# Reordering the opening of a fused retention and GELU kernel, and starting one attention stage a unit of the first layer later

## The chip, the cores and the metric

One core of one Trainium2 chip. The metric is the time of one execution in microseconds (us) on the device. A trace gives the span from the first to the last instruction; it is 1.6 to 1.9 us shorter than the time of the same execution.

## The reference, cut to what matters

```python
# attention: q, k, v of shape (4, 8, 768, 64), a decayed running state for each head
for t in range(S):
    state = gamma * state + einsum('bhd,bhe->bhde', k[:, :, t], v[:, :, t])
    y[:, :, t] = scale * einsum('bhd,bhde->bhe', q[:, :, t], state)
x = y.transpose(0, 2, 1, 3).reshape(3072, 512)
# then a two-layer network with w_in (512 x 2048) and w_out (2048 x 512)
h = x @ w_in
out = gelu_tanh(h) @ w_out
```

The kernel cuts the sequence into six chunks of 128 steps. In each chunk there are four tiles, one for each of the four batches. For a tile it computes: transposes of q and k (T), the masked products of k and q (A), the chunk's output y from A and v plus the old state times q, and the new state s. The four tiles of a chunk then go through the first layer (M1, into banks called h), GELU on ScalarE, and the second layer (M2, into banks called o). While a chunk is in M1 and M2, the attention of the next chunk is woven in between.

## The kernel before

The parts that the argument needs, with cuts marked:

```python
    def prep1(eng, nm, c, b):          # decay factors times q or k, or a plain cast of v, to fp16
        ...
    BANKS = {"h": 2, "o": 2, "att": 4} # PSUM banks of each kind
    ...
    def spin(n, tag="h"):              # products of zeros, to keep TensorE busy
        ps = bank(tag, shape=(128, 512), name="spin_ps")
        for _ in range(n):
            nc.tensor.matmul(out=ps, lhsT=zero[:, 0:128], rhs=zero, start=True, stop=True)
    ...
    # loads of chunk 0: q, k, v of four tiles from the queues of SyncE and ScalarE; then, in program order:
    spin(14)
    prep1(VE, "q", 0, 0)
    prep1(PO, "k", 0, 0)               # GpSimd
    mm_T(0, 0)
    ev_T(0, 0, AC)                     # eviction on ScalarE
    load1(AC, "v", 0, 2)
    prep1(VE, "q", 0, 1)
    prep1(PO, "k", 0, 1)
    prep1(PO, "k", 0, 2)

    load_w_in(0)                       # first w_in block, half of the contraction each,
    load_w_in(1)                       # both issued by GpSimd, behind its k of tile 2
    prep1(PO, "k", 0, 3)
    ... # further w_in, w_out; then A, y, T, A ... of tiles 0 to 3 with spins between
    t01, t23 = (0, half), (half, 2 * half)
    m1a = [moe1_parts(0, fp, *t01) for fp in range(2)]
    m1a[0](range(2))                   # M1 of tiles 0 and 1, first half of the contraction: load_w_in(0)
    ...
    m1a[0](range(2, 4))                # second half: needs load_w_in(1)
    m1a[1](range(2, 4))
    for b in range(2):
        ev_S(0, b)
        moe1_two(0, b, *t23)           # M1 of tiles 2 and 3, in an h bank
        mm_s(0, 2 + b)
    ...
    # SyncE's loads of chunk 1 begin when w_out part 2 has landed (hold), all in one queue:
    hold("q", 1, 1, w_out_sb[2][0:1, 0, 0:1])
    ...
    for b in range(B):
        load1(SY, "k", 2, b)
    load_blk("q", 2)                   # sixteen transfers: q of chunk 2, all tiles
    ...
    for nm in "kqv":                   # GpSimd: k of chunk 2, then q, then v
        for b in range(B):
            prep_blk("q", 2, b) if nm == "q" else prep1(PO, nm, 2, b)
    # M1 of chunk 1, sixteen units; after unit n comes the attention of chunk 2:
            8: [(att_T, 2, 0), (load, 3)],
            10: [(att_T, 2, 1)],
            13: [(att_AY, 2, (), "att", 2, (0, 1), None)],   # A of tiles 0 and 1
```

Of the kernel before, what the change touches and what calls it, by code (L numbers as in the profile page):

```python
# [16 lines left out]
def kernel(  # L17
# [40 lines left out]
    att = ctx.enter_context(tc.tile_pool(name="att", bufs=4))  # L58
# [30 lines left out]
    def ld_tile(nm, c, b):  # L89
        if nm == "q":  # L90
            t = ld_all(("q32", c)).rearrange("p (b hp) a d -> p b (hp a d)", b=B)
            return t[:, b].rearrange("p (h d) -> p h d", h=H)
        if (nm, c, b) not in raw:
            raw[nm, c, b] = ld.tile([128, H, Dh], F32, tag=f"{nm}32", bufs=6, name=f"{nm}32")
        return raw[nm, c, b]
# [72 lines left out]
    def spin(n, tag="h"):  # L168
        ps = bank(tag, shape=(128, 512), name="spin_ps")
        for _ in range(n):  # L170
            nc.tensor.matmul(  # L171
                out=ps, lhsT=zero[:, 0:128], rhs=zero, start=True, stop=True
            )
# [9 lines left out]
    def prep1(eng, nm, c, b):  # L183
        t = pre.tile(
            [128, H, Dh], F16, tag=f"{nm}16", bufs=6 if nm == "q" else 2 * B, name=f"{nm}16"
        )
        src = ld_tile(nm, c, b)
        if nm == "v":
            if eng is nc.scalar:
                eng.copy(out=t, in_=src)  # L190
            else:
                eng.tensor_copy(out=t, in_=src)
        else:
            col = OQ if nm == "q" else OK
            eng.tensor_tensor(  # L195
                out=t,
                in0=src,
                in1=cst[:, col:col + H].unsqueeze(2).broadcast_to([128, H, Dh]),
                op=ALU.mult,
            )  # L200
        h16[nm, c, b] = t
# [12 lines left out]
    def pair(t, hp):  # L214
        return t[:, 2 * hp:2 * hp + 2]
# [6 lines left out]
    def copy_on(eng, out, in_):  # L222
        if eng is nc.scalar:
            eng.copy(out=out, in_=in_)  # L224
        else:
            eng.tensor_copy(out=out, in_=in_)  # L226
# [5 lines left out]
    def bank(tag, dt=F32, shape=(128, NHP, 128), name="ps"):  # L232
        return psum.tile(list(shape), dt, tag=tag, bufs=BANKS[tag], name=name)

    def mm_T(c, b):
        parts = [(i, nm) for i, nm in enumerate("qk") if c not in BLK[nm]]
        if not parts:
            return
        ps = bank("att", F16, (128, 2, NHP, 128), "qkT_ps")
        for i, nm in parts:  # L240
            for hp in range(NHP):
                nc.tensor.transpose(  # L242
                    out=ps[:, i, hp], in_=pair(h16[nm, c, b], hp), identity=iden
                )
        pss["T", c, b] = ps

    def ev_T(c, b, eng=nc.vector):
        t = att.tile([128, 2, NHP, 128], F16, tag="qkT", name="qkT")
        for i, nm in enumerate("qk"):
            if c in BLK[nm]:  # L250
                nc.vector.transpose(  # L251
                    out=t[:, i].rearrange("p hp t -> p (hp t)"),
                    in_=blk16.pop((nm, c, b)).rearrange("p ha d -> p (ha d)"),
                )
        if ("T", c, b) in pss:
            i0 = sum(c in BLK[nm] for nm in "qk")
            copy_on(eng, t[:, i0:], pss.pop(("T", c, b))[:, i0:])
        qkT[c, b] = t

    def mm_A(c, b):  # L260
        t = qkT[c, b]
        ps = [bank("att", name=f"a_ps{j}") for j in range(2)]
        for hp in range(NHP):
            for j in range(2):
                nc.tensor.matmul(  # L265
                    out=ps[j][:, hp],
                    lhsT=t[j * 64:(j + 1) * 64, 1, hp],
                    rhs=t[j * 64:(j + 1) * 64, 0, hp],
                    start=True,
                    stop=True,  # L270
                )
        pss["A", c, b] = ps

    def ev_A(c, b):
        ps = pss.pop(("A", c, b))
        for j in range(2):
            s = att.tile([128, NHP, 128], F16, tag=f"a{j}", name=f"a_sb{j}")
            nc.vector.tensor_tensor(out=s, in0=ps[j], in1=mask[:, j], op=ALU.mult)  # L278
            a_sb[c, b, j] = s

    def mm_yc(c, b, tag):
        y_ps = pss["Y", c, b] = bank(tag, name="y_ps")
        if c == 0:
            return

        for hp in range(NHP):
            nc.tensor.matmul(  # L287
                out=y_ps[:, hp],
                lhsT=st[:, hp, b],
                rhs=qkT[c, b][:, 0, hp],  # L290
                start=(hp == 0),
                stop=False,
                skip_group_check=True,
            )

    def mm_yi(c, b):
        y_ps = pss["Y", c, b]
        for hp in range(NHP):
            for j in range(2):
                nc.tensor.matmul(  # L300
                    out=y_ps[j * 64:(j + 1) * 64, hp],
                    lhsT=h16["v", c, b][:, 2 * hp + j],
                    rhs=a_sb[c, b, j][:, hp],
                    start=(c == 0),
                    stop=True,
                    skip_group_check=True,
                )

    def ev_Y(c, b, eng=nc.vector):
        if c not in xT:  # L310
            xT[c] = xp.tile([128, NHP, B * C], F16, tag="x", name="xT")
        copy_on(eng, xT[c][:, :, b * C:(b + 1) * C], pss.pop(("Y", c, b)))

    def mm_s(c, b, tag="att"):
        if c + 1 >= NCk:
            return
        s_ps = pss["S", c, b] = bank(tag, name="s_ps")
        for hp in range(NHP):
            nc.tensor.matmul(  # L319
                out=s_ps[:, hp],  # L320
                lhsT=pair(h16["k", c, b], hp),
                rhs=pair(h16["v", c, b], hp),
                start=True,
                stop=True,
            )
# [97 lines left out]
    def moe1_mm(c, fc, out, t0, t1, kcs=range(NHP), first=True):  # L423
        for kc in kcs:
            nc.tensor.matmul(  # L425
                out=out,
                lhsT=w_in_of(fc, kc),
                rhs=xT[c][:, kc, t0:t1],
                start=(kc == 0 and first),
                stop=(kc == NHP - 1),  # L430
                skip_group_check=True,
            )

    def g_tile(c, fc):
        if (c, fc // 2) not in g_sb:
            g_sb[c, fc // 2] = gp.tile([128, 2, B * C], F16, tag=f"g{fc // 2}", name="g")
        return g_sb[c, fc // 2]

    def gelu(out, in_):
        nc.scalar.activation(out=out, in_=in_, func=AF.Gelu_apprx_tanh, scale=1.0)  # L440
# [6 lines left out]
    def moe1_two(c, fp, t0, t1, tag="h"):  # L447

        h_ps = bank(tag, shape=(128, 2, B * C // 2), name="h_ps")
        for r in range(2):  # L450
            moe1_mm(c, 2 * fp + r, h_ps[:, r, 0:t1 - t0], t0, t1)
        gelu(g_tile(c, 2 * fp)[:, :, t0:t1], h_ps[:, :, 0:t1 - t0])
# [64 lines left out]
    VE, AC, PO, SY = nc.vector, nc.scalar, nc.gpsimd, nc.sync  # L517
# [4 lines left out]
    load1(AC, "k", 0, 3)  # L522
    spin(14)
    prep1(VE, "q", 0, 0)
    prep1(PO, "k", 0, 0)
    mm_T(0, 0)
    ev_T(0, 0, AC)
    load1(AC, "v", 0, 2)
# [18 lines left out]
    spin(3)  # L547
    mm_A(0, 1)
    ev_A(0, 1)
    prep1(AC, "v", 0, 1)  # L550
    prep1(VE, "q", 0, 3)
    mm_yc(0, 0, "o")
    mm_yi(0, 0)
    ev_Y(0, 0, AC)
    spin(4)
    mm_yc(0, 1, "o")
    mm_yi(0, 1)
    ev_Y(0, 1, AC)
    mm_T(0, 2)
    ev_T(0, 2)  # L560
    mm_T(0, 3)
    ev_T(0, 3, AC)
    mm_A(0, 2)
    ev_A(0, 2)
    prep1(AC, "v", 0, 2)
    prep1(AC, "v", 0, 3)
    spin(3)
    mm_A(0, 3)
    ev_A(0, 3)


    t01, t23 = (0, half), (half, 2 * half)
    m1a = [moe1_parts(0, fp, *t01) for fp in range(2)]
    m1a[0](range(2))
    mm_yc(0, 2, "o")
    mm_yi(0, 2)
    ev_Y(0, 2, AC)
    m1a[1](range(2))
    mm_s(0, 0)
    mm_s(0, 1)  # L580
    mm_yc(0, 3, "o")
    mm_yi(0, 3)
    ev_Y(0, 3)
    m1a[0](range(2, 4))
    m1a[1](range(2, 4))
    for b in range(2):
        ev_S(0, b)
        moe1_two(0, b, *t23)
        mm_s(0, 2 + b)
    ev_S(0, 2)  # L590
    ev_S(0, 3)
# [52 lines left out]
    for nm in "kqv":  # L644
        for b in range(B):
# [11 lines left out]
            6: [(att_S, 1, 3)],  # L657
            8: [(att_T, 2, 0), (load, 3)],
            10: [(att_T, 2, 1)],
            13: [(att_AY, 2, (), "att", 2, (0, 1), None)],  # L660
            14: [(att_T, 2, 2)],
            15: [(att_T, 2, 3)],
        },
    )
    run(
        [x for b in range(B) for x in units2(1, b)],
        {
            1: [(att_AY, 2, (), "att", 2, (2, 3), None)],
            4: [(att_Y, 2)],
            6: [(att_S, 2, 0)],  # L670
            7: [(att_S, 2, 1)],
            8: [(att_S, 2, 2)],
            9: [(att_S, 2, 3)],
        },
    )

# [60 lines left out]
```

## Time and profile before

| | before |
|---|---|
| time, median of 3 | 213.74 us (213.71 to 213.85) |
| span of the traced execution (its time 214.22 us) | 212.4 us |
| TensorE busy | 205.6 us, 97% |
| spins | 28 matmuls of 128x512 zeros |
| first 128x512 row of M1 / first matmul of M2 | 21.50 / 31.86 us |
| last matmul ends | 208.58 us |

How to read it: TensorE is the bound, and its matmuls stand in program order, so time can only be won where TensorE waits or spins. The view of waits lists the waits by what ended them; the timeline shows when each group of matmuls started. The page and the lines that matter are shown in the prediction below. The **chain that ended last** follows, from the last instruction backwards, what released each step; where it leaves TensorE, something else sets the pace. And a **landing** is the moment when the last of a transfer's sixteen parts has signalled (the records hold sixteen signals for a transfer). The **relay** is the opening's chain of handoffs: TensorE's products, their eviction by ScalarE or VectorE, and the next products that need them.

### The profile page before, as it was taken

To read this page: it belongs to the slowest core of one execution; us is meant where nothing else is said; L and a number is where in the kernel's file an instruction comes from. 1 tells how busy PE (TensorE), PEld (TensorE's weight loads), DVE (VectorE), ACT (ScalarE), POOL (GpSimd) and SP (SyncE) were. 2 spreads that over 40 slices of the span, in tenths; PEclk is the share of its full clock that TensorE was granted. 3 is DMA by queue.
4 is the path that set the end of the run, shared out by engine and by line. 5 is a ranking of instruction groups with operands and counts; after the bars stand their busy time and mean duration, and the time that the engine had idled before them with its cause. 6 is when DMAs were issued, how large, how long until landed. Compare 5 with 4: busy or idle time off the path is not lost.

```text
span 212.4 us, 3868 instructions
## 1 busy us (share of the span) xinstructions
PE 205.6 (97%) x1516; PEld 111.3 (52%) x1516; DVE 89.2 (42%) x161; ACT 84.2 (40%) x141; POOL 95.8 (45%) x117
## 2 busy tenths in 40 slices
PE   7989999999999999999999999999999999999992
PEld 2457444457897564444464444464444464444461
DVE  5478201198619753365544365544355520100001
ACT  2374661255455131465131465131465131565110
POOL 2796400513819418599309599301599301100000
PEclk9999999999999999999999999999999999999999
DMA  6999999999789788979789996879910012100121
GB/s 157 288 250 207 206 203 233 241 241 231 127 222 224 112 161 159 252 177 175 120 162 190 303 192 103 124 153 241 281 34 3 0 49 102 49 0 0 49 92 59
DMA packets 124289, 32.78 MB, mean 154 GB/s; under 512 B 118064, under 2 KB 122416, under 8 KB 124272
## 3 DMA queue, kind: packets, MB, share of 16 engines
q1 hardware_dynamic: 108880, 20.75, 49.4%
q0 software_dynamic: 5600, 8.65, 17.2%
q10 hardware_dynamic: 9792, 3.15, 6.1%
q8 instruction: 12, 0.20, 0.4%
q14 instruction: 5, 0.04, 0.1%
HBM read 30.44 MB, written 6.29 MB: 173 GB/s over the span
## 4 chain that ended last, share of the span: by engine, by line
PE 87%; SPq 4%; DVE 2%; DMA 2%; ACT 1%; issue 1%; POOL 0%; POOLq 0%
PE o_ps L470 39%; PE h_ps L425 34%; SPq L110 4%; PE spin_ps L171 4%; PE a_ps L265 3%; PE y_ps L300 3%; PE y_ps L287 2%; DMA q<-in_q_dram 2%; PE s_ps L319 2%; PE qkT_ps L242 2%; ACT qkT L224 1%; DVE qkT L226 1%; DVE qkT L251 1%; POOL q L206 0%; DVE q L195 0%
## 5 line engine op out<-in xcount | busy, mean ns | idle before, releaser
L470 PE MATMUL o_ps<-w_out,g 128*128 128x512 f16 (+1 forms) x400 | 88.1, 371 | 0.0
L425 PE MATMUL h_ps<-xT,w_in 128*128 128x512 f16 (+1 forms) x464 | 86.8, 342 | 0.3 <-ACT g L440 0.2
L440 ACT ACTIVATE g<-h_ps 128x512 f16<-128x512 f32 x96 | 57.2, 597 | 47.8 <-PE h_ps L425 47.8
L425 PEld LDWEIGHTS <-w_in 128*128 128x128 f16 x464 | 44.4, 98 | 37.9 <-issue 0.3
L470 PEld LDWEIGHTS <-g 128*128 128x128 f16 x400 | 37.7, 98 | 38.8
L278 DVE TENSOR_TENSOR a_sb<-a_ps,mask 128x512 f16<-128x512 f32 x48 | 30.0, 682 | 15.9 <-PE a_ps L265 15.8
L492 ACT COPY o_sb<-o_ps 128x512 f32<-128x512 f32 x19 | 11.1, 586 | 54.3 <-PE o_ps L470 49.9
L497 POOL DMA_DIRECT2D out_dram<-o_sb x17 | 9.6, 564 | 46.9 <-ACT o_sb L492 35.0
L195 POOL TENSOR_TENSOR k<-k,cst 128x512 f16<-128x512 f32 x24 | 24.7, 1036 | 11.9 <-DMA k<-in_k_dram 11.8
L345 POOL TENSOR_TENSOR stg<-st,cst 128x512 f32<-128x512 f16 x16 | 16.3, 1041 | 11.5 <-DVE st L336 9.5
L206 POOL TENSOR_TENSOR q<-q,cst 128x512 f16<-128x512 f32 x16 | 16.6, 1048 | 5.2 <-DMA q<-in_q_dram 5.1
L336 DVE TENSOR_TENSOR st<-s_ps,stg 64x256 f16<-64x256 f32 x32 | 13.5, 422 | 7.8 <-PE s_ps L319 7.3
L251 DVE STREAM_TRANSPOSE qkT<-q 128x512 f16<-128x512 f16 x16 | 11.3, 706 | 11.7 <-POOL q L206 11.7
L195 DVE TENSOR_TENSOR q<-q,cst 128x512 f16<-128x512 f32 x8 | 6.3, 781 | 17.2 <-DMA q<-in_q_dram 17.2
L206 POOL TENSOR_TENSOR kT<-kT,cst 128x512 f16<-128x512 f32 x12 | 12.5, 1044 | 0.0
L226 DVE CAST xT<-y_ps 128x512 f16<-128x512 f32 x11 | 7.2, 686 | 11.9 <-PE y_ps L300 11.9
L508 DVE COPY o_sb<-o_ps 128x256 f32<-128x256 f32 x2 | 0.8, 424 | 26.6 <-PE o_ps L470 26.6
L224 ACT CAST xT<-y_ps 128x512 f16<-128x512 f32 x13 | 7.2, 588 | 9.9 <-PE y_ps L300 9.9
L171 PE MATMUL spin_ps<-zero 128*128 128x512 f16 x28 | 9.6, 499 | 1.3 <-DVE zero L139 1.3
L490 DVE COPY o_sb<-o_ps 128x512 f32<-128x512 f32 x4 | 2.8, 691 | 19.0 <-PE o_ps L470 14.7
L265 PE MATMUL a_ps<-qkT 64*128 64x128 f16 x192 | 8.3, 218 | 1.3 <-ACT qkT L224 0.7
L251 DVE STREAM_TRANSPOSE qkT<-kT 128x512 f16<-128x512 f16 x12 | 8.4, 700 | 2.6 <-POOL kT L206 2.6
(32 smaller groups left out, 98.2 us busy)
## 6 DMA issues: line engine op xcount, KB each, us to landing
v<-in_v_dram SPq DMA_DIRECT2D x22, 256.0 KB, 4.4
k<-in_k_dram SPq DMA_DIRECT2D x20, 256.0 KB, 4.9
out_dram<-o_sb POOLq DMA_DIRECT2D x17, 256.0 KB, 3.2
q<-in_q_dram SPq DMA_DIRECT2D x64, 64.0 KB, 2.7
kT<-in_k_dram SPq DMA_DIRECT2D x48, 64.0 KB, 2.7
w_out<-in_moe_w_out_dram POOLq DMA_DIRECT2D x4, 512.0 KB, 15.5
w_in<-in_moe_w_in_dram POOLq DMA_DIRECT2D x3, 512.0 KB, 8.9
q<-in_q_dram SPq DMA_DIRECT2D x5, 256.0 KB, 6.1
```

The costliest lines, as they stand in the source:

```text
L171: nc.tensor.matmul(out=ps, lhsT=zero[:, 0:128], rhs=zero, start=True, stop=True)
L195: eng.tensor_tensor(out=t, in0=src, in1=cst[:, col:col + H].unsqueeze(2).broadcast_to([128, H, Dh]), op=ALU.mult,)
L206: nc.gpsimd.tensor_tensor(out=t, in0=ld_all((key, c))[:, b * NHP:(b + 1) * NHP].rearrange("p hp a d -> p (hp a) d"), in1=cst[:, col:col + ...
L251: nc.vector.transpose(out=t[:, i].rearrange("p hp t -> p (hp t)"), in_=blk16.pop((nm, c, b)).rearrange("p ha d -> p (ha d)"),)
L265: nc.tensor.matmul(out=ps[j][:, hp], lhsT=t[j * 64:(j + 1) * 64, 1, hp], rhs=t[j * 64:(j + 1) * 64, 0, hp], start=True, stop=True,)
L278: nc.vector.tensor_tensor(out=s, in0=ps[j], in1=mask[:, j], op=ALU.mult)
L336: eng.tensor_tensor(out=st[sl, :, b, sl], in0=s_ps[sl, :, sl], in1=stg[sl, :, b, sl], op=ALU.add,)
L345: nc.gpsimd.tensor_tensor(out=stg[:, :, b], in0=st[:, :, b], in1=cst[:, OG:OG + NHP].unsqueeze(2).broadcast_to([128, NHP, 128]), op=ALU.mult,)
L425: nc.tensor.matmul(out=out, lhsT=w_in_of(fc, kc), rhs=xT[c][:, kc, t0:t1], start=(kc == 0 and first), stop=(kc == NHP - 1), skip_group_che ...
L440: nc.scalar.activation(out=out, in_=in_, func=AF.Gelu_apprx_tanh, scale=1.0)
L470: nc.tensor.matmul(out=ps[:, n0:n1], lhsT=g_sb[c, fc // 2][:, fc % 2, b * C:(b + 1) * C], rhs=w_out_sb[fc // (NF // NO)][:, fc % (NF // NO ...
L492: nc.scalar.copy(out=o_sb, in_=ps)
```

## The change

Three parts: (1) k of tile 0 is prepared on VectorE instead of GpSimd; (2) the opening is reordered: T of tile 2 goes ahead of y of tile 1, A of tile 2 ahead of T of tile 3, the s tiles are spread out, the spins are dealt anew (30 instead of 28), and M1 of tiles 2 and 3 takes one o bank so that it needn't wait for a GELU; (3) A of chunk 2, tiles 0 and 1, goes behind unit 14 of M1 instead of unit 13, and all that follows in chunk 2 moves along.

```diff
@@ -522,7 +522,7 @@
     load1(AC, "k", 0, 3)
     spin(14)
     prep1(VE, "q", 0, 0)
-    prep1(PO, "k", 0, 0)
+    prep1(VE, "k", 0, 0)
     mm_T(0, 0)
     ev_T(0, 0, AC)
     load1(AC, "v", 0, 2)
@@ -547,45 +547,46 @@
     spin(3)
     mm_A(0, 1)
     ev_A(0, 1)
-    prep1(AC, "v", 0, 1)
-    prep1(VE, "q", 0, 3)
     mm_yc(0, 0, "o")
     mm_yi(0, 0)
     ev_Y(0, 0, AC)
-    spin(4)
+    prep1(AC, "v", 0, 1)
+    mm_T(0, 2)
+    ev_T(0, 2)
+    spin(3)
     mm_yc(0, 1, "o")
     mm_yi(0, 1)
     ev_Y(0, 1, AC)
-    mm_T(0, 2)
-    ev_T(0, 2)
+    mm_A(0, 2)
+    prep1(VE, "q", 0, 3)
+    ev_A(0, 2)
+    spin(2)
     mm_T(0, 3)
     ev_T(0, 3, AC)
-    mm_A(0, 2)
-    ev_A(0, 2)
+    spin(4)
+    mm_A(0, 3)
+    ev_A(0, 3)
     prep1(AC, "v", 0, 2)
     prep1(AC, "v", 0, 3)
-    spin(3)
-    mm_A(0, 3)
-    ev_A(0, 3)
+    mm_yc(0, 2, "o")
+    mm_yi(0, 2)
+    ev_Y(0, 2, AC)
 
 
     t01, t23 = (0, half), (half, 2 * half)
     m1a = [moe1_parts(0, fp, *t01) for fp in range(2)]
     m1a[0](range(2))
-    mm_yc(0, 2, "o")
-    mm_yi(0, 2)
-    ev_Y(0, 2, AC)
+    mm_s(0, 0)
     m1a[1](range(2))
-    mm_s(0, 0)
-    mm_s(0, 1)
     mm_yc(0, 3, "o")
     mm_yi(0, 3)
     ev_Y(0, 3)
     m1a[0](range(2, 4))
+    mm_s(0, 1)
     m1a[1](range(2, 4))
     for b in range(2):
         ev_S(0, b)
-        moe1_two(0, b, *t23)
+        moe1_two(0, b, *t23, "oh"[b])
         mm_s(0, 2 + b)
     ev_S(0, 2)
     ev_S(0, 3)
@@ -657,20 +658,19 @@
             6: [(att_S, 1, 3)],
             8: [(att_T, 2, 0), (load, 3)],
             10: [(att_T, 2, 1)],
-            13: [(att_AY, 2, (), "att", 2, (0, 1), None)],
-            14: [(att_T, 2, 2)],
-            15: [(att_T, 2, 3)],
+            14: [(att_AY, 2, (), "att", 2, (0, 1), None)],
         },
     )
     run(
         [x for b in range(B) for x in units2(1, b)],
         {
-            1: [(att_AY, 2, (), "att", 2, (2, 3), None)],
-            4: [(att_Y, 2)],
-            6: [(att_S, 2, 0)],
-            7: [(att_S, 2, 1)],
-            8: [(att_S, 2, 2)],
-            9: [(att_S, 2, 3)],
+            0: [(att_T, 2, 2), (att_T, 2, 3)],
+            3: [(att_AY, 2, (), "att", 2, (2, 3), None)],
+            7: [(att_Y, 2)],
+            9: [(att_S, 2, 0)],
+            10: [(att_S, 2, 1)],
+            11: [(att_S, 2, 2)],
+            12: [(att_S, 2, 3)],
         },
     )
 
```

## The prediction

> **What bounds the kernel now.** I read the page first, busy shares and then the chain that ended last.
>
> ```profile
> PE 205.6 (97%) x1516; PEld 111.3 (52%) x1516; DVE 89.2 (42%) x161; ACT 84.2 (40%) x141; POOL 95.8 (45%) x117
> PE o_ps L470 39%; PE h_ps L425 34%; SPq L110 4%; PE spin_ps L171 4%; PE a_ps L265 3%; PE y_ps L300 3%; PE y_ps L287 2%; DMA q<-in_q_dram 2%; PE s_ps L319 2%; PE qkT_ps L242 2%; ACT qkT L224 1%; DVE qkT L226 1%; DVE qkT L251 1%; POOL q L206 0%; DVE q L195 0%
> ```
>
> TensorE is busy 97% of the 212.4 us span, and no other engine is over half. The change removes no matmul that the result needs, so it can only win where TensorE waits or spins (spin_ps is a product of zeros, made to keep the array busy). The view of waits, for TensorE alone, is the whole list of such places:
>
> ```profile
> PE spin_ps L171 <- DVE zero L139: 1.3, 1, 1.3
> PE a_ps L265 <- ACT qkT L224: 0.7, 2, 0.5
> PE a_ps L265 <- DVE qkT L226: 0.6, 2, 0.3
> PE h_ps L425 <- ACT g L440: 0.2, 1, 0.2
> ```
>
> That is 2.8 us, of which the first 1.3 is the launch and untouched. So 2.8 us of waits and the 28 spins are all there is; 2% of the time would be 4.3 us. The timeline of TensorE in the opening shows where each wait lies (start, length, work, then the idle time before it in brackets):
>
> ```profile
> 1.26 5.94 PE L171 MATMUL spin_ps<-zero 128*128 128x512 f16 x14 [1.26 <-DVE zero L139]
> 7.04 0.39 PE L242 MATMUL qkT_ps<-iden,q 128*128 128x128 f16 x4
> 7.26 0.39 PE L242 MATMUL qkT_ps<-iden,k 128*128 128x128 f16 x4
> 7.48 1.03 PE L171 MATMUL spin_ps<-zero 128*128 128x512 f16 x4
> 8.75 0.40 PE L265 MATMUL a_ps<-qkT 64*128 64x128 f16 x8 [0.24 <-ACT qkT L224]
> 10.80 0.40 PE L265 MATMUL a_ps<-qkT 64*128 64x128 f16 x8 [0.46 <-ACT qkT L224]
> 14.39 0.40 PE L265 MATMUL a_ps<-qkT 64*128 64x128 f16 x8 [0.34 <-DVE qkT L226]
> 15.47 0.40 PE L265 MATMUL a_ps<-qkT 64*128 64x128 f16 x8
> 19.32 1.03 PE L425 MATMUL h_ps<-xT,w_in 128*128 128x256 f16 x8 [0.25 <-ACT g L440]
> ```
>
> The first transposes (7.04) begin when the fourteen spins are out, not when q and k are ready. From there the opening is a relay: transposes, eviction, A, eviction, y. The last of the 128x512 rows of M1 begins at 21.50; from there TensorE waits once more only, in the middle of the kernel:
>
> ```profile
> 64.76 0.42 DVE L226 COPY qkT<-qkT_ps 128x512 f16<-128x512 f16 x1
> 65.10 0.70 DVE L251 STREAM_TRANSPOSE qkT<-q 128x512 f16<-128x512 f16 x1
> 65.73 0.38 DVE L226 COPY qkT<-qkT_ps 128x512 f16<-128x512 f16 x1
> 66.17 0.40 PE L265 MATMUL a_ps<-qkT 64*128 64x128 f16 x8 [0.30 <-DVE qkT L226]
> ```
>
> Here A of chunk 2, tile 1, waits for a copy that ends at 66.11.
>
> The preparations concerned are these rows of the timeline:
>
> ```profile
> 3.88 0.69 DVE L195 TENSOR_TENSOR q<-q,cst 128x512 f16<-128x512 f32 x1 [0.35 <-DMA q<-in_q_dram]
> 5.74 2.04 POOL L195 TENSOR_TENSOR k<-k,cst 128x512 f16<-128x512 f32 x2 [2.11 <-DMA k<-in_k_dram]
> 7.39 0.94 DVE L195 TENSOR_TENSOR q<-q,cst 128x512 f16<-128x512 f32 x1 [2.81 <-DMA q<-in_q_dram]
> ```
>
> **What the Trainium skill says.** (1) "TensorE: Matmul & The Clock Gate", section "Wait — 56ns, not 53.3ns?": matmuls of 512 columns follow one another at 426.7 ns while the array is cold and 215.7 ns when warm. The trace agrees: weight loads of the first spins are 0.43 us apart, and the later group of four (1.03 us, last one 0.38) gives (1.03 - 0.38)/3 = 0.217. (2) Same page, "What's actually happening": the full clock is granted after a busy window of about 3.4 us, and the window runs free of the kernel's start. Here thirteen cold spins take 13 x 0.427 = 5.55 us, to 6.81, and the fourteenth only 0.23, so the grant came at about 6.8; no run yet shows whether other executions differ. (3) "GPSIMD Engine Reference", 3.1: tensor_tensor is 1.96 times slower on GpSimd than on VectorE at fp32. Here 1.04 against 0.69, a factor of 1.5. (4) "SBUF — State Buffer", "Who interferes with whom": a VectorE instruction with two SBUF inputs contends with a GpSimd one that reads SBUF. Agrees: the q preparation that overlapped GpSimd took 0.94, the one alone 0.69.
>
> **Part 1, first k on VectorE.** k lands at 5.7. On GpSimd it is ready at 5.74 + 1.02 = 6.76, on VectorE at about 5.74 + 0.69 = 6.43: 0.33 us earlier. But the spins hold the transposes until 7.04, so in an execution like the profiled one this is worth 0.00. Where the clock comes earlier, the spins end earlier: with a grant r us after the first spin they end at 1.26 + 14 x 0.216 + 0.494 r = 4.28 + 0.494 r (estimate), 5.96 at r = 3.4. There the k preparation decides, and up to 0.33 is won. If half of the executions were so I would count 0.1 on average. I choose 0.08.
>
> **Part 2, order of the opening.** I walked the new program order with these steps, all read from the timeline: eight transposes 0.44 us of TensorE, A 0.33, y 0.35, s of one tile 0.23, four M1 matmuls of 256 columns 0.44, a spin 0.216; from the last matmul to the start of its eviction 0.20; eviction of 128x1024 on ScalarE 1.01, on VectorE 0.69; 128x512 on ScalarE 0.57; two A evictions on VectorE 1.29; from the end of an eviction to the matmul that needs it 0.06.
> Up to A of tile 1 (10.80) nothing moves. y of tile 0 starts at 11.32 as before (its v ends at 11.22). Transposes of tile 2 follow at 11.67; VectorE evicts them after A of tile 1 (busy to 12.5), to 13.14. ScalarE now takes xT of tile 0 (11.84 to 12.43) ahead of v of tile 1, which ends at 12.95, so y of tile 1 starts at 13.0 (before: 12.63). A of tile 2 at 13.35, with its operand ready: the wait of 14.39 is gone, and that A is 1.04 us earlier. Then two spins to 14.10, transposes of tile 3 to 14.56, ScalarE evicts 14.76 to 15.77, four spins to 15.42, A of tile 3 at 15.83: 0.36 us later than before, because its eviction takes 1.01 and begins later. ScalarE then prepares v 2 (to 16.24), so y of tile 2 at 16.30, M1 first halves and s of tile 0 to 17.76, y of tile 3 at 17.76 to 18.11, M1 second halves and s of tile 1 to 19.22. M1 of the second pair of tiles takes an M2 bank that was freed at 17.4, so the wait of 19.32 is gone, as are the 0.2 us that the overlap of matmul drain hides in that row (18.89 to 19.32 is 0.43 of issue time). It ends, with s of tiles 2 and 3, at 21.41, against 21.50. **Gain 0.09 us.**
> Check by the sum: TensorE's issue gaps from 7.04 to 21.50 are now 0.41, 0.61, 0.20, 0.10, 0.49, 0.11, 0.10, 0.09 and 0.43 = 2.54; after, 0.41, 0.61, 0.20, 0.23, 0.41 and 0.14 = 2.00. That is 0.54 less, but the spins go from 28 to 30, two at 0.216 = 0.43. The difference is 0.11.
>
> **Part 3, A of chunk 2 one tile on.** Another M1 unit of eight 256-column matmuls (0.87) goes ahead of the A pair. It would start at about 66.3, its operand is ready at 66.17: the wait, 65.80 to 66.17 of issue time, is gone: **0.37 us**. The transposes of tiles 2 and 3, moved behind the first M2 unit, start near 68.7; VectorE, after four A evictions, is done with them at about 70.8, and their A comes near 71.8. Y of chunk 2 then comes near 76, its A evictions end at about 74.5. The s tiles come three units (2.6 us) later, to about 84; GpSimd's decays then end near 85.5, and its preparations of chunk 3 start only at 87.89 now. So no new wait. Beside other work and worth nothing: all VectorE and GpSimd times here.
>
> **Sum.** 213.74 - 0.08 - 0.09 - 0.37 = 213.20 us.
>
> **Rivals.**
> (a) The relay takes the gain back or worse: v of tile 1 behind xT, and A of tile 3 behind a ScalarE eviction, hold the end of the opening. For: my walk shows 0.36 us lost at A of tile 3. Against: later rows are then free of waits. With steps 0.1 longer in three places the opening would lose 0.2 to 0.3: 213.5.
> (b) The first k does matter: in unprofiled executions the clock is granted early, k bounds, and 0.33 passes down the whole relay. For: GpSimd is ready only 0.28 before the spins end. Against: the three timed runs lie within 0.14 us, so phases hardly scatter: 212.9.
> (c) The later A, Y and s of chunk 2 press on chunk 3 (decays, banks). For: they are moved by 2.6 us. Against: GpSimd idles 3.0 us before 87.33. It would take back the 0.37: 213.6.
> (d) VectorE becomes late with q of tile 1, as k comes ahead of it. Against: that q lands at 7.39, k would be done at 6.43; it may even go from 0.94 to 0.69. 0.0.
>
> **Range and chances.** Middle 213.2. The error of the walk is some 0.3 to 0.4 either way (nine handoffs), the clock phase 0.3 to the fast side, (c) 0.4 to the slow side; together 212.6 to 213.8. Faster than 209.5 would need 4.3 us, more than every TensorE wait together: 0.01. Slower than 218.0 would need a lost clock or a long stall: 0.01.
>
> **What would show it.** Right: first transposes still at spin's end, near 7.0; A of tile 2 near 13.4 with no wait for VectorE; A of tile 3 near 15.8 with a wait for ScalarE of some 0.2 to 0.3; no wait for g; the 128x512 rows of M1 starting at 21.3 to 21.5; no wait for qkT near 66. Wrong: first transposes before 6.8, or a start of those rows outside 20.9 to 21.8, or a new TensorE wait after 22 us, in particular in front of A, y or s of chunks 2 and 3.

## The result, and the profile after

The first comparison gave 213.83 us (213.11 to 213.97, 4 runs) against 213.73 us before (213.60 to 213.85, 4 runs). A ratio here is the mean time of one kernel's runs over that of the other's in the same rounds, so it is not quite the ratio of the medians quoted. This one is 0.9998, with a 95% interval of 0.9974 to 1.0021. Two more comparisons of the same kernel, made later and told below, gave 0.9965 (0.9948 to 0.9983) and 0.9970 (0.9951 to 0.9989). So the change is worth between nothing and some 0.7 us, and less than 2% in any case.

The page of after, with busy times and the chain that ended last:

```profile
PE 204.6 (96%) x1518; PEld 111.1 (52%) x1518; DVE 89.6 (42%) x162; ACT 84.2 (40%) x141; POOL 94.8 (45%) x116
PE o_ps L470 40%; PE h_ps L425 39%; DMA w_in<-in_moe_w_in_dram 3%; DMA k<-in_k_dram 3%; PE a_ps L265 3%; PE y_ps L300 3%; PE y_ps L287 2%; PE s_ps L319 2%; PE qkT_ps L242 1%; SPq L98 1%; POOL k L195 0%; POOL w_in L409 0%; DVE o_sb L508 0%; SPq L126 0%
```

Before, the chain held the spins (4%) and the queue that issues q loads (SPq L110, 4%). Now it holds a w_in transfer. The waits of TensorE:

```profile
PE a_ps L265 <- ACT qkT L224: 1.3, 3, 0.6
PE spin_ps L171 <- DVE zero L139: 1.3, 1, 1.3
PE h_ps L425 <- DMA w_in<-in_moe_w_in_dram: 0.7, 1, 0.7
```

The waits for VectorE's qkT and for ScalarE's g are gone, as intended. In their place stands a wait that was not there before: 0.7 us for w_in. The timeline of TensorE in the opening shows where:

```profile
1.25 4.84 PE L171 MATMUL spin_ps<-zero 128*128 128x512 f16 x14 [1.25 <-DVE zero L139]
5.93 0.39 PE L242 MATMUL qkT_ps<-iden,q 128*128 128x128 f16 x4
7.99 0.40 PE L265 MATMUL a_ps<-qkT 64*128 64x128 f16 x8 [0.59 <-ACT qkT L224]
10.04 0.40 PE L265 MATMUL a_ps<-qkT 64*128 64x128 f16 x8 [0.46 <-ACT qkT L224]
12.52 0.40 PE L265 MATMUL a_ps<-qkT 64*128 64x128 f16 x8
15.01 0.40 PE L265 MATMUL a_ps<-qkT 64*128 64x128 f16 x8 [0.24 <-ACT qkT L224]
18.14 0.61 PE L425 MATMUL h_ps<-xT,w_in 128*128 128x256 f16 x4 [0.65 <-DMA w_in<-in_moe_w_in_dram]
21.44 2.75 PE L425 MATMUL h_ps<-xT,w_in 128*128 128x512 f16 x12
```

The spins end 1.1 us earlier than in the trace of before. That is not the change: the full clock was granted at 4.6 us here and at 6.9 us there, before the first instruction that the change touches (k on VectorE, at 5.24 us); and e2 below, with the old opening, got it at 4.39. With it every step of the relay is earlier, A of tile 2 by 1.87 us. But the second half of M1 starts at 18.14, where it started at 18.02 before, and the 128x512 rows at 21.44 instead of 21.50. All that the opening had won was waited off at one place. The chain that ended last, in order of time (start, length, what), says what that place hangs on:

```profile
2.36 6.42 DMA k<-in_k_dram
8.85 1.04 POOL k L195
10.72 7.36 DMA w_in<-in_moe_w_in_dram
```

k of tile 2 lands, GpSimd prepares it, then issues the second half of the first w_in block, and that takes 7.36 us to land. None of this is touched by the new order. In the middle of the kernel, the copy on VectorE

```profile
65.51 0.39 DVE L226 COPY qkT<-qkT_ps 128x512 f16<-128x512 f16 x1
```

is now done before TensorE comes to it, and both A follow without a gap:

```profile
66.27 0.62 PE L265 MATMUL a_ps<-qkT 64*128 64x128 f16 x16
```

### The profile page after: what moved, and what is told of

Read it like the earlier page. It is cut to its first block, busy times and chain, and to the rows that moved or that the text cites. A ratio compares the mean times of both kernels' runs of the same rounds, so it can differ in the third digit from the quotient of the medians.

```text
span 212.0 us, 3873 instructions
## 1 busy us (share of the span) xinstructions
PE 204.6 (96%) x1518; PEld 111.1 (52%) x1518; DVE 89.6 (42%) x162; ACT 84.2 (40%) x141; POOL 94.8 (45%) x116
## 3 DMA queue, kind: packets, MB, share of 16 engines
q0 software_dynamic: 5600, 8.65, 17.1%
## 4 chain that ended last, share of the span: by engine, by line
PE 90%; DMA 7%; POOL 1%; SPq 1%; DVE 0%; issue 0%
PE o_ps L470 40%; PE h_ps L425 39%; DMA w_in<-in_moe_w_in_dram 3%; DMA k<-in_k_dram 3%; PE a_ps L265 3%; PE y_ps L300 3%; PE y_ps L287 2%; PE s_ps L319 2%; PE qkT_ps L242 1%; SPq L98 1%; POOL k L195 0%; POOL w_in L409 0%; DVE o_sb L508 0%; SPq L126 0%
## 5 line engine op out<-in xcount | busy, mean ns | idle before, releaser
L278 DVE TENSOR_TENSOR a_sb<-a_ps,mask 128x512 f16<-128x512 f32 x48 | 30.1, 683 | 17.5 <-PE a_ps L265 17.5
L195 POOL TENSOR_TENSOR k<-k,cst 128x512 f16<-128x512 f32 x23 | 23.7, 1035 | 12.3 <-DMA k<-in_k_dram 12.3
L336 DVE TENSOR_TENSOR st<-s_ps,stg 64x256 f16<-64x256 f32 x32 | 13.5, 421 | 7.8 <-PE s_ps L319 7.3
L171 PE MATMUL spin_ps<-zero 128*128 128x512 f16 x30 | 9.1, 444 | 1.3 <-DVE zero L139 1.3
L192 POOL CAST v<-v 128x512 f16<-128x512 f32 x16 | 9.5, 602 | 0.0
```

Source lines behind the costliest of these rows:

```text
L192: eng.tensor_copy(out=t, in_=src)
L195: eng.tensor_tensor(out=t, in0=src, in1=cst[:, col:col + H].unsqueeze(2).broadcast_to([128, H, Dh]), op=ALU.mult,)
L278: nc.vector.tensor_tensor(out=s, in0=ps[j], in1=mask[:, j], op=ALU.mult)
L336: eng.tensor_tensor(out=st[sl, :, b, sl], in0=s_ps[sl, :, sl], in1=stg[sl, :, b, sl], op=ALU.add,)
```

## The experiments

**The theories.** *Theory R* (my prediction): the opening is a relay of evictions between TensorE, ScalarE and VectorE, and the middle wait is a fixed 0.37 us, so the parts add up. *Theory W*: the end of the opening is set by the landing of the second half of the first w_in block. *Theory M*: the wait in the middle is the end of a chain of loads that runs on its own time, so that whatever TensorE wins earlier only makes that wait longer. *Theory N*: plain noise.

To keep them apart I read the same marks from every trace: when the clock was granted, when TensorE's first 16 KB instruction fetch started during the run, when the second half of the first w_in block had landed, when M2's first matmul started, and when the last matmul ended. The last column is the difference of the two before it: all that TensorE does after the opening.

```
kernel                    clock   fetch   w_in landed   M2 starts   last matmul   after the opening
before                     6.86   16.35      16.71        31.86       208.58         176.72
e0 before again            7.01   16.58      16.76        31.94       208.81         176.87
e10 before, q ahead        7.05   16.75      16.63        31.97       208.23         176.26
e2 part 3 alone            4.39   16.36      16.80        31.57       207.80         176.23
e3 parts 1 and 2 alone     4.86   16.01      16.74        31.02       209.42         178.40
e8 e3, q ahead             4.31   15.94      17.98        31.69       207.95         176.26
after                      4.62   16.02      18.09        31.80       208.03         176.23
e1 after again             5.50   16.16      18.20        31.91       208.16         176.25
e14 after, third time      5.26   15.86      16.66        31.05       207.65         176.60
e9 after, q ahead          4.37   15.89      17.97        31.68       207.91         176.23
e4 after, fewer spins      6.72   17.29      16.76        31.51       207.82         176.31
e11 e9, fewer spins        5.81   16.68      16.46        31.11       207.35         176.24
e13 e11 again              4.97   16.56      16.70        30.94       207.18         176.24
e12 e9, w_in early         4.32   16.07      15.95        34.88       211.12         176.24
```

In ten of the fourteen traces, with very different openings, the rest takes 176.23 to 176.31 us, and in none of these ten does TensorE's view of waits hold an entry after the opening. So each trace can be taken apart into an opening and a surplus over 176.24.

And the times, each with its own runs of before on the same chip:

| run | median, us | before, us | ratio | 95% interval |
|---|---|---|---|---|
| e0 before against itself | 213.99 | 214.16 | 0.9991 | 0.9972 to 1.0010 |
| e1 after | 213.43 | 214.16 | 0.9965 | 0.9948 to 0.9983 |
| e2 part 3 alone | 213.29 | 214.16 | 0.9956 | 0.9937 to 0.9974 |
| e3 parts 1 and 2 alone | 214.10 | 214.16 | 1.0000 | 0.9976 to 1.0023 |
| e4 after, nine spins fewer | 213.78 | 214.06 | 0.9991 | 0.9968 to 1.0015 |
| e8 e3 with q ahead | 213.53 | 214.06 | 0.9970 | 0.9954 to 0.9987 |
| e9 after with q ahead | 213.49 | 214.06 | 0.9968 | 0.9951 to 0.9986 |
| e10 before with q ahead | 213.62 | 214.06 | 0.9974 | 0.9956 to 0.9991 |
| e11 e9, nine spins fewer | 212.89 | 213.72 | 0.9963 | 0.9945 to 0.9980 |
| e12 e9, w_in early | 216.42 | 213.72 | 1.0109 | 1.0080 to 1.0137 |
| e13 e11 again | 212.92 | 214.22 | 0.9950 | 0.9928 to 0.9972 |
| e14 after, third time | 213.54 | 214.22 | 0.9970 | 0.9951 to 0.9989 |

All gave correct results.

### e0 and e1: both kernels again

No edit in either.

> The kernel before, submitted against itself, as a control: ratio 1.000 with an interval of some 0.2%. Its first trace came from an execution of 214.22 us, 0.5 us above the timed ones, with TensorE's clock granted at 6.8 us; theory W (the second half of the first w_in block, which TensorE needs at about 18.0 us, sets the end of the opening) expects this trace to reach the first 128x512 rows of M1 at 21.2 to 21.5 us whatever its clock does; theory R (the relay of evictions sets it) expects that start to move with the clock, by up to 0.8 us earlier when the clock comes at 4.6.

> The kernel after once more. Theory W: the first 128x512 rows of M1 start at about 21.4 us again if one part of w_in lands late (18.1 us, when a 16 KB instruction fetch falls on the same DMA engine), and at about 20.7 us in executions where it does not; spans then scatter over 211.3 to 212.3 us, in two groups. Theory N (plain noise): spans scatter evenly and w_in lands at the same time in all traces. Theory R: the start of M1's rows follows the clock grant alone. The ratio to before is 0.997 to 1.000.

The control came out at 0.9991, so differences below 0.2% are not told apart by timing. Its trace again had a late clock (7.01) and M2 starting at 31.94, so it could not tell theories W and R apart. e1 came out at 0.9965. Its clock came at 5.50, yet M2 started at 31.91, no earlier than in e0: w_in had landed only at 18.20. That is against theory R, for which the opening should have moved with the clock. The two groups of spans that I expected don't show: e1's six lie evenly from 211.5 to 212.1. For the landing itself theory N is out: w_in landed at 16.5 to 16.8 or at 18.0 to 18.2 in all traces but e12's, whose loads are reordered, and nowhere between.

### e2 and e3: the change cut in two

e2 is the kernel before with the last hunk of the diff. e3 is the kernel after without it.

> The kernel before with the third part alone (A of chunk 2 one tile on). My prediction counted 0.37 us: ratio 0.9983, and no TensorE wait for qkT near 66 us. The rival that later work presses on chunk 3 expects 1.000 with a new wait after 80 us.

> The kernel after without its third part: opening and first k alone. Theory W: 1.000 within 0.001 when w_in is late (gain 0.1 us), 0.9965 when it is not. Theory R (my prediction): 0.9992, 0.17 us. If the opening loses time, it is above 1.001. The wait for qkT near 66 us is back, 0.3 us.

e2 gave 0.9956, which is 0.9 us where I had counted 0.37. e3 gave 1.0000, where I had counted 0.17 us. Together (e1, same chip) they gave 0.9965. The parts do not add up in the way of the prediction: as far as the intervals tell, all of the gain is in part 3 (e3's runs from 0.9976 to 1.0023).

e3's trace is the most instructive of all. Its opening is the one that was hoped for: w_in landed at 16.74, and M2 started at 31.02, 0.8 us before the first trace of before. Parts 1 and 2 together do win something in such a trace: e14 came to 31.05 in the same way, while e2, with the old opening, an early clock too (4.39) and w_in at 16.80, came to 31.57. And yet e3's last matmul ended at 209.42, later than before. This is what TensorE waited for between 60 and 70 us:

```profile
PE a_ps L265 <- DVE qkT L226: 1.6, 2, 1.0
```

In the first trace of before that line says 0.3, 1, 0.3. The chain that ended last shows the middle of before and of e3 in the same terms. First before:

```profile
58.75 3.79 DMA q<-in_q_dram
62.93 1.06 POOL q L206
65.80 0.32 DVE qkT L226
66.17 0.40 PE a_ps L265 x8
```

Then e3:

```profile
63.79 1.04 POOL q L206
66.58 0.38 DVE qkT L226
67.01 0.40 PE a_ps L265 x8
```

In both, the last q load of chunk 2, GpSimd's preparation, VectorE's transpose and copy, and A of tile 1 follow one another without slack. (In e3 the view names a store ahead of GpSimd, out_dram; the last q load landed at 63.38, and GpSimd began 0.40 us later, as in before, where it was 0.39.) In e3, TensorE is 0.8 us ahead when it leaves the opening, but q is 0.86 us later. The loads do not follow TensorE: they begin when w_out part 2 has landed (33.2 us before, 33.8 in e3) and then run through one queue, in which each issue begins within 0.05 us of the end of the one before. In the eight traces with the loads in the old order the last q load landed at 62.3 to 62.8, and at 63.38 in e3 alone, while M2 started anywhere from 31.02 to 31.94. This is theory M.

The chain view puts the release of the first q load down to VectorE, "DVE st L336" in before. That can't be what it waits for: in e10 below, with the same program for VectorE, the same load was let go three VectorE instructions sooner (the view names a_sb L278). By the program it waits only for the readers of its buffer, q of chunk 0, done by 13.1 us in before.

(The traced execution of e3 was its slowest, 215.11 us, with a surplus of 2.16 us over 176.24; its median equals that of before. I take from it where the gain went, not how much goes there on average.)

### e8, e9 and e10: the q loads of chunk 2 moved ahead

If the chain of loads is the pace of the middle, moving the loads must release what the opening won, without touching the order of TensorE. The edit is the same for all three kernels:

```diff
-    for b in range(B):
+    for b in range(2):
         load1(SY, "k", 2, b)
     load_blk("q", 2)
+    for b in range(2, B):
+        load1(SY, "k", 2, b)
...
-    for nm in "kqv":
-        for b in range(B):
-            prep_blk("q", 2, b) if nm == "q" else prep1(PO, nm, 2, b)
+    # (shortened) GpSimd: k0, k1, q0 to q3, k2, k3, v0 to v3
```

> Opening and first k alone (e3), with the sixteen q loads of chunk 2 issued ahead of the last two k loads, and prepared ahead of those two k. Theory M (the load chain of chunk 2 sets when A of chunk 2, tile 1, can start, at 66.1 to 67.0 us, and TensorE's earlier arrival only lengthens that wait): the copy is ready some 1.5 us earlier, the wait near 66 us is gone, and the total falls from 1.000 (e3) to 0.994 to 0.996. Theory R (opening gain was lost inside the opening): no change, 1.000, or only the 0.3 us of the wait in before, 0.9985.

> The kernel after with the same reordered loads. Theory M: in after the A was already moved behind the copy, so this gives little: 0.995 to 0.9965, like after (0.9965), unless the opening comes out early, then down to 0.993.

> The kernel before with the same reordered loads and nothing else. Theory M: it removes the same wait that the third part of the change removes, so it should equal that part alone (e2: 0.9956): 0.995 to 0.997. Theory that the third part gained by something else than the wait for the q load (fewer switches, other bank use): 0.999 to 1.000.

With e3's opening and the loads ahead, the ratio went from 1.0000 to 0.9970. The copy of tile 1 is done at 63.22 (in e3 it started at 66.57):

```profile
62.84 0.38 DVE L226 COPY qkT<-qkT_ps 128x512 f16<-128x512 f16 x1
```

and the waits of TensorE in e8 hold no qkT from VectorE any more:

```profile
PE spin_ps L171 <- DVE zero L139: 1.3, 1, 1.3
PE a_ps L265 <- ACT qkT L224: 1.1, 3, 0.5
PE h_ps L425 <- DMA w_in<-in_moe_w_in_dram: 0.8, 1, 0.8
```

e10 is the kernel before with this edit alone: 0.9974, just outside the 0.995 to 0.997 that I expected; its interval, up to 0.9991, still touches the rival's 0.999, so the trace has to decide. It has a surplus of 0.02 us instead of 0.5 to 0.6. Its copy is early and both A follow without a gap:

```profile
63.06 0.42 DVE L226 COPY qkT<-qkT_ps 128x512 f16<-128x512 f16 x1
65.57 0.62 PE L265 MATMUL a_ps<-qkT 64*128 64x128 f16 x16
```

So an edit that moves no TensorE instruction does the work of part 3. That settles theory M: part 3 gains by no longer standing in front of the q loads. It also explains why the parts do not add: e8, e9 and e10, all free of that chain, lie within 0.0006 (0.1 us) of each other: with the chain of loads out of the way, and w_in late in the traces of e8 and e9, the opening is worth so little that timing can't tell it from nothing. I had hoped for more from e8 (0.994 to 0.996). The missing part is in the last line above: w_in was late again (17.98), and M2 started at 31.69.

### e4: the fetch moved, first attempt

The late landings of w_in have a pattern. In the trace of after, fifteen of the sixteen parts had landed by 16.79 us and the last came at 18.09. A 16 KB instruction fetch, one packet, ran from 16.02 to 16.91, and the last of the sixteen small packets that end this w_in transfer started at 16.90. The same holds in e1, e8 and e9: the last small packet started between 0.02 us before and 0.16 us after the end of the fetch, the other fifteen by 16.44 at the latest. In e3 and e14 the fetch came as early, but all sixteen had started by 16.38. The record does not name a packet's engine; that the fetch sat on the engine of the late part is my inference. The Trainium skill's page "Runtime: NRT & Kernel Launch", section "Instruction fetch mechanics", says that the sequencer fetches its instructions itself, in blocks of 16 KiB or 256 instructions, through a DMA queue of its own, and that the cost is mostly hidden. The trace agrees with the size: twelve such packets of 16384 bytes in after, against TensorE's 3036 instructions, 253 each. If the fetch comes at the wrong moment it may hold up a part of w_in. So I took nine spins out of after, to have it come 18 instructions later:

```diff
     ev_T(0, 2)
-    spin(3)
...
     ev_A(0, 2)
-    spin(2)
...
     ev_T(0, 3, AC)
-    spin(4)
```

> The kernel after without nine of its spins (three behind the transposes of tile 2, two ahead of those of tile 3, four ahead of A of tile 3): TensorE has 18 instructions fewer there, so its first 16 KB instruction fetch comes later, near 16.6 us instead of 16.0 to 16.2, when the second half of the first w_in block has landed. Theory W: no wait for w_in near 18 us, M2's first matmul at 31.0 to 31.2 us (31.8 to 31.9 in both traces of after), and a wait for qkT from VectorE comes back near 66 us, as TensorE arrives there before the copy is ready; the total is then 0.994 to 0.997 of before. Rival, the relay needs the spins' clock: the grant lapses and M2 begins after 32 us.

The fetch came at 17.29 and w_in was complete at 16.76, without a wait. But the traced execution had a late clock (6.72), so the opening was late for another reason, M2 started at 31.51 instead of 31.0 to 31.2, and the times scattered from 213.51 to 214.53 with a ratio of 0.9991. The wait for qkT near 66 us that I expected back is not there. As a test of theory W this one is inconclusive, and I can't say why its mean is no better than that of after.

### e11 and e13: the fetch moved, with the q loads ahead

Based on e9. Nine spins are taken out in another way, so that no gap of the relay is left without one:

```diff
-    spin(4)   # behind T of tile 0
+    spin(2)
-    spin(3)   # behind T of tile 1
+    spin(1)
-    spin(3)   # behind T of tile 2
+    spin(1)
-    spin(2)   # ahead of T of tile 3
+    spin(1)
-    spin(4)   # ahead of A of tile 3
+    spin(2)
```

> The kernel after with the reordered q loads of chunk 2 (e9) and nine of the sixteen later spins taken out, each group keeping at least one: 18 TensorE instructions fewer, so the first 16 KB instruction fetch should come after 16.4 us instead of 15.9 to 16.2. Theory W: the second half of the first w_in block lands complete by 16.8 us, no wait for w_in, M2's first matmul at 30.9 to 31.2 us where the clock comes early (31.7 in e9's trace), and with the q loads ahead nothing near 66 us takes it back: 0.992 to 0.994 of before. Rivals: the straggling part of w_in has another cause than the fetch, then w_in still lands at 18.0 and the ratio stays at 0.997; or fewer spins cost the clock and it is slower than e9.

> The kernel of e11 (after, q loads of chunk 2 ahead, nine spins fewer) on the same chip as the kernel after, to compare them directly: theory W and M together expect 0.995 to 0.9965 of before and at least 0.3 us less than after; first fetch after 16.4 us, no wait for w_in, M2 at 31.0 to 31.2 us. If it is not below after, the gain of e11's trace is not kept in most executions.

The fetch came at 16.68 and 16.56, w_in was complete at 16.46 and 16.70, M2 started at 31.11 and 30.94. The waits of TensorE in e11 hold neither w_in nor VectorE:

```profile
PE a_ps L265 <- ACT qkT L224: 2.2, 3, 0.9
PE spin_ps L171 <- DVE zero L139: 1.3, 1, 1.3
PE y_ps L300 <- ACT v L190: 0.4, 1, 0.4
```

and the second half of M1 starts 0.7 us earlier than in after:

```profile
17.45 0.61 PE L425 MATMUL h_ps<-xT,w_in 128*128 128x256 f16 x4
```

The waits for ScalarE are longer than in after (2.2 against 1.3 us), because the spins that had filled them are gone, and M2 starts no later for it. e11 gave 0.9963 and e13 0.9950. On the same chip e13 took 212.92 us, after 213.54 us (e14) and before 214.22 us: five of e13's six runs are below all six of e14's. So this version beats both kernels. How much of the 0.6 us against after is due to the spins and how much to the loads is not separated: e9 was not run on that chip. Taking out spins also changes more than the time of the fetch. I had expected more of e11 by the ratio (0.992 to 0.994); the trace's opening came as expected, the mean did not fall as far.

### e12: the w_in loads moved ahead

The opposite way to have w_in in time: issue its two halves before GpSimd's preparation of k of tile 2.

```diff
     prep1(PO, "k", 0, 1)
-    prep1(PO, "k", 0, 2)
-
     load_w_in(0)
     load_w_in(1)
+    prep1(PO, "k", 0, 2)
```

> e9 with the two halves of the first w_in block issued from GpSimd ahead of its preparation of k of tile 2, so some 2 us earlier (near 7.5 us instead of 9.8). Theory W: both halves land by about 15.5 us, before the fetch, so the wait for w_in near 18 us is gone: M2 begins at 31.0 to 31.3 us, ratio 0.993 to 0.995. Rival: the loads of v and q share the same saturated DMA engines and come as much later, the relay waits for v of tiles 2 and 3, and M2 begins at 31.7 or later, ratio 0.997 or above.

The rival was right, and by more than it asked: 1.0109. w_in landed at 15.95, but v of tiles 2 and 3 only at 17.1 and 17.3 instead of 13.1 and 14.0 in e9, and TensorE stood for them:

```profile
PE y_ps L300 <- ACT v L190: 2.2, 1, 2.2
```

Just after that wait, which ended at 17.82, the clock was lost, too: the records show it granted at 4.32, taken back at 17.98 and granted again at 21.39, and the four M1 matmuls that follow took 1.03 us instead of 0.61. In the opening the DMA engines never rest (203 to 289 GB/s in every 2 us from 4 to 22 us in after), and here the transfer put ahead pushed the others back.

### e14: after for the third time

No edit; it was run beside e13.

> The kernel after, on the same chip as e13: 0.9965 to 0.9998 of before, as in its two earlier comparisons; where its clock comes before 6 us, the fetch at 15.9 to 16.2 us and the second half of the first w_in block late, at 18.0 to 18.2 us; where it comes at 6.8 us, the fetch later and w_in at 16.7 us.

0.9970. The traced execution had an early clock (5.26) and a fetch at 15.86, and yet w_in was complete at 16.66 and M2 started at 31.05. So half of the expectation failed: a fetch between 15.86 and 16.16 goes with a late w_in in four of six traces (after, e1, e8, e9; not e3, e14), not in all; e12 is left out, as its w_in had landed before the fetch. With the fetch at 16.35 or later, w_in was in time in all seven traces. And with this good opening, TensorE met later stages too early even in after: the surplus was 0.36 us instead of 0. Matched matmul by matmul with the first trace of after, 0.21 us of it goes in the attention of chunk 1 between 43 and 45 us, where a q preparation on VectorE took 1.33 us beside GpSimd's k instead of 0.68, and 0.14 at A of chunk 2, tile 1, near 66 us.

## Why the prediction was right or wrong

- **The bound, and the size of the whole.** It said that TensorE's own waits and spins limit the gain to far less than 2%, and 213.20 us in all, 0.54 us less than before. Three comparisons gave 0.9998, 0.9965 and 0.9970, that is 0.04, 0.75 and 0.64 us, taken on 214 us. The bound is right, and the size fits two of the three; the first, with a median of 213.83, sits at the edge of the stated 212.6 to 213.8. The way to it was wrong in the two steps that follow: 0.17 for the opening, which gave 0.00, and 0.37 for part 3, which gave 0.94. One was too high, the other too low; that the sum came near is in part luck.
- **The sum (failed).** I added 0.08, 0.09 and 0.37 us as if each wait could be removed by itself. The opening alone gave 0.00 (e3), part 3 alone 0.94 us (0.0044 of 214.16; e2), both together 0.75. The wait at 66 us is the end of a chain of loads that begins with the landing of w_out part 2. An earlier TensorE stands there longer, and once that place is relieved, earlier slack can show at once. I had the chain before my eyes: the page's chain gives 4% to SPq L110, the issue of these q loads, and 2% to DMA of q. I read it as a share and did not ask what it hangs on. Followed back by the profile alone, it leads by way of VectorE to TensorE's transposes at 47.4; only the comparison of traces, told at e3, shows that nothing in it depends on TensorE.
- **Part 3, its term.** The mechanism (A waits for the copy, one unit more gives it time) was right; the term was too small. Two A that run back to back start 0.24 us apart (66.27 and 66.51 in after); in before they start 0.70 apart, so the gap is 0.46, not 0.37, and the surplus over 176.24 is 0.48 in that trace and 0.63 in e0. In the traces, e2's last matmul ended 1.01 us before e0's: 0.64 from the surplus and 0.37 from an opening with an earlier clock. By theory M, before would have lost these 0.37 again at 66 us, and so the rest of the 0.94 would be explained; but no trace of before has an early clock, so this is not shown.
- **Part 2, the relay.** The walk itself held. From A of tile 1 to A of tile 2 I had 2.55 us, measured 2.48; from A of tile 1 to A of tile 3, 5.03 against 4.97. The step that failed is the one behind it, the second halves of M1 to 19.22: I took them to start as soon as y of tile 3 was issued (7.31 us after A of tile 1; so in e11, 7.16), and never looked up when their w_in lands. In after they waited for it, to 18.14. The bank move worked: the wait for g is in no trace of after. That the 128x512 rows came at 21.44, inside my 21.3 to 21.5, is luck: A of tile 1 was 0.76 us earlier than in the walk, by the clock, and the wait for w_in took 0.65 back.
- **Part 1.** I put it at 0 when the clock comes late and up to 0.33 us when early, and took half of the executions as early (half of 0.33 is 0.17, not the 0.1 or the 0.08 that I put down). One of my signs of being wrong came true here: the first transposes of after began at 5.93, before 6.8, by the early clock of rival (b). In the traces the clock came anywhere between 4.3 and 7.1 us, in ten of fourteen before 6 us. In e2, with k on GpSimd and the clock at 4.39, A of tile 0 started at 7.99; in e8 and e9, with k on VectorE and nearly the same clock, at 7.67 and 7.75. So some 0.3 is seen in these single traces. But in after it started at 7.99 as well: its eviction on ScalarE waited to 6.92, as ScalarE was issuing a k load until 6.88. And in e8 and e9 what passed was waited off at w_in (0.8 us each). No part of the measured gain can be put down to it.
- **Rivals.** (c), later work of chunk 2 pressing on chunk 3, was rightly put low: no TensorE wait after 22 us in after, and 176.23 us behind the opening. (d) was right to be nothing. (a) had the right outcome, the opening's gain given back, by a cause it did not have: a transfer, not a handoff. (b) was half right on the clock, and its reason against, a scatter of only 0.14 us, was too few runs: in a later comparison eleven runs of before lie between 213.83 and 215.01.

**What stays open.** The late landing of w_in is shown; that the instruction fetch causes it is argued, from the small packets that start as the fetch ends in four traces and from a rule that eleven of thirteen traces follow (late where the fetch starts by 16.16, in time where it starts at 16.35 or later), and not shown: e4, e11 and e13 moved the fetch by taking out spins, which changes TensorE's own times too. Nor is it known why the late part, in after, landed 1.19 us after its small packet started. Why the first comparison gave 0.9998 and the later ones 0.997 is not settled either; their intervals overlap.

## What to carry to other kernels

When TensorE is 97% busy and its few waits are short, ask of each wait what the last step of it hangs on, and whether that moves when TensorE comes earlier. If it is a chain of loads on its own time, gains ahead of it may be worth nothing (here 1.0000 in e3) and must not be added; move the load, or move the work that waits for it. And before an opening is tightened, look up when each of its transfers lands: here, in four of the traces, w_in landed at 18.0 to 18.2, when even the old opening wanted it at 18.02.

## What the Trainium skill lacked or had wrong

- "TensorE: Matmul & The Clock Gate", section "What you observe": it gives about 4 us of matmuls, within 500 ns from run to run, to the full clock. Here the grant came between 3.05 and 5.79 us after the first matmul in fourteen traces of kernels that all begin with the same spins, so the spread is near 2.7 us, and the 500 ns does not hold. The next section's own note, that one kernel was measured with 6, 11 or 14 cold matmuls, agrees better: here, at 0.427 us a spin, the grant falls after some 7 to 14 of them.
- "Runtime: NRT & Kernel Launch", section "Instruction fetch mechanics": the cost of a block boundary is called mostly hidden. No page gives the time of a fetch or what it can cost a load that runs beside it. Here one fetch took 0.89 to 0.98 us, and in four of six traces with the fetch at 15.86 to 16.16 us one part of a load landed 1.3 to 1.6 us after the other fifteen.
- "GPSIMD Engine Reference", section 3.1: the factor of 1.96 against VectorE is for 2048 fp32 elements. For 512 elements with fp16 output it was 1.04 to 0.69 us, 1.5.
